# Linear attention into a soft mixture of experts on one core: a batch's second half in other PSUM banks, a batch's keys one tile later, and the drain's zero products in another bank

## The chip, the cores and the metric

The kernel runs on one core of one Trainium2 chip. The metric is device microseconds (us) of one execution. All inputs and the output are float32 and lie in HBM. The host only rearranges the inputs before the launch and the output after it; all arithmetic is on the core.

## The reference

The first part is linear attention without a softmax, for 8 batches and 8 heads, with 576 positions and a head width of 64. Its output is normalised per position and head. The second part is a soft mixture of 8 experts with 4 slots each (32 slots) over all 4608 rows of 512 values.

```python
kv  = einsum('bhsd,bhse->bhde', k, v)
out = einsum('bhsd,bhde->bhse', q, kv)
x   = out / sqrt(mean(out*out, -1) + 1e-6) * g_norm      # to 4608 x 512
logits = x @ phi                                          # 4608 x 32
d = exp(logits - logits.max(0)); d /= d.sum(0)            # over rows
slot_in  = d.T @ x                                        # 32 x 512
slot_out = relu(slot_in[e] @ w1[e]) @ w2[e]               # 4 slots of each expert
c = exp(logits - logits.max(1)); c /= c.sum(1)            # over slots
result = c @ slot_out
```

The softmax over rows needs the maximum of each slot's column over all 4608 rows, so the slot inputs are complete only when the last row tile has its logits. The experts can't start before that.

## The kernel before

**Loads.** All loads and stores are issued by SyncE (SP) in one order: per batch two 1 MB tiles of keys and values (`kv`, L59), 256 KB with the last 64 positions (`kvr`, L63), then the queries (`q`, L70; `qr`, L68), then the expert weights `w1` (L86; some in four parts, L82) and `w2` (L91). The 1 MB tiles share a ring of 17 buffers (`ring`), so a later weight load waits in SP's queue until the tile that used its buffer has been consumed: the weights of experts 6 and 7 and the late halves of `w2` take buffers of the first experts' weights. Each load also uses one of eight completion semaphores in turn, so a load isn't issued before the one eight places ahead of it has landed.

**Stage 1, the row tiles.** The loop over `T` takes 36 tiles of 128 rows, nine for two batches. `products(T)` (L211) multiplies the queries by a block-diagonal matrix `bd` of the batch (there are two, `bds[0]` and `bds[1]`, for even and odd batches) into a PSUM tile `o` of two banks; there are two such tiles under the tag `o`. ScalarE (ACT) squares and evicts it (L237, L244, L245), VectorE (DVE) reduces (L250, L304) and does a Newton step (L266 to L268), GpSimd (POOL) scales (L277, L299). Two tiles make a stage; six tiles make a group, whose column maximum (L317), spread over partitions by TensorE (`pm`, L327) and reduced (L333), feeds the running softmax (`pb`, L342; `d`, L348 and L349) and the weighted sums `pS` (L361).

**The keys.** `class Kv` (L142) makes `bd` of one batch: products of keys and values (L159), the last 64 positions (L174), a copy to SBUF (`kvT`, L183), a transpose and a product with phi (L188, L190), and copies into `bd` (L194 on ACT; L202 on DVE for batch 0, L204 on ACT for the others). All of it uses one PSUM tile of two banks under the tag `kv`, of which there is one. Batch 0 is made ahead of the loop in two halves `g`, each from one of its 1 MB tiles. For every other batch the three steps of `kv_step` (L374) are spread over three iterations: products of the first tile, products of the second tile with the last positions, then the transposes and copies. They stand ahead of `products(T)` in the iterations `first[b] - 3` to `first[b] - 1`. For batch 1 `first` is 4, so these are iterations 1, 2 and 3.

**Order.** The schedule is the program order on each engine; nothing reorders it. Every engine works through its own list, so an instruction that waits holds all that stand behind it on that engine.

**The drain.** After the loop the last two tiles `A` and `Z` go through with smaller steps (L455 to L517). The last group's maximum is the gate: L317 on DVE, `pm` on TensorE, `rmax` (L333) on DVE, `diag` (L337) on ACT, `pb`, `d`, `pS`, the accumulator (L368), its transpose `psT` (L501), `sTe` (L505), then the first expert product `ph` (L564). `tail_ps` is a PSUM tile of two banks under the tag `kv`; the roots of the last two stages are kept in its first bank.

**Zero products.** `fill(n)` (L396) puts `n` bf16 products of zeros, 128 by 256, on TensorE; nobody reads them. They stand at the start (`EARLY`) and in the drain (`LATE_FILL`). Before the drain they go to a new tile of tag `o`; in the drain to the second bank of `tail_ps`. The tag `m` is one bank, used in turn by `pm`, `pb` and `psT`.

**Stage 2.** Experts (L559, L578), the combine weights on DVE (L535), then for each of two halves of the columns a mixing step (L594) and six output tiles (L603), each stored by one DMA of 768 KB (L621).

Of the kernel before, what the change touches and what calls it, by code (L numbers as in the profile page):

```python
# [8 lines left out]
F32 = mybir.dt.float32  # L9
# [5 lines left out]
P = 128  # L15
B, H, S, D = 8, 8, 576, 64
# [9 lines left out]
CT = 12  # L26
NCH = NT // CT
NX = 14
EARLY = (18, 2, 2)
LATE_FILL = (24, 5, 5, 2, 2)  # L30
PACED = 3
SLOT = 2048
NSLOT = 17
# [8 lines left out]
def soft_moe_linear_attention(ctx: ExitStack, tc: tile.TileContext, kv_in, kvr_in, q_in, qr_in, w1_in, w2_in, c_in, out):  # L42


    nc = tc.nc
# [61 lines left out]
    zeros = const.tile([P, 256], BF16, name="zeros")  # L107
# [17 lines left out]
    for i in range(NX):  # L125
        t = const.tile([P, 4, 129], F32, name=f"x{i}")
# [12 lines left out]
    ps = psA.enter_context(tc.tile_pool(name="psA", bufs=1, space=bass.MemoryType.PSUM))  # L139


    class Kv:  # L142


        def __init__(self, b):
            self.b = b
            self.bd = bds[b % 2]
            t = ps.tile([P, 2, 512], F32, tag="kv", name=f"kvp{b}")
            self.pkv = t[:, :, :128].rearrange("p w (g d) -> p w g d", g=2)
            self.pT = t[:, 0, 128:384].rearrange("p (g n) -> p g n", g=2)  # L150
            self.pM = t[:, 1, 128:384].rearrange("p (g h w n) -> p g h w n", g=2, h=2, w=2)

        def products(self, r):
            g, w = divmod(r, 2)
            main = kv_sb[self.b, g].rearrange("p (r w c n) -> p r w c n", r=2, w=2, c=4)
            for c in range(4):
                for i in range(2):
                    lo = 64 * i
                    nc.tensor.matmul(  # L159
                        self.pkv[lo : lo + 64, w, g],  # L160
                        lhsT=main[:, w, 1, c, lo : lo + 64],
                        rhs=main[:, w, 0, c, lo : lo + 64],
                        start=c == 0 and (g == 0 or self.b == 0),
                        stop=False,
                    )
# [66 lines left out]
    def square(T, o):  # L232
        s = stage_of[T]
        if T == starts[s]:
            sqs[s] = wk.tile([P, STAGES[s], 4, P], F32, tag="sq", name=f"sq{s}")

        nc.scalar.activation(sqs[s][:, T - starts[s]], o[:, :, 32:160], AF.Square, scale=0.125)  # L237

    def evict(T, o):
        s = stage_of[T]  # L240
        if T == starts[s]:
            parts[s] = wk.tile([P, STAGES[s], H, NS], F32, tag="part", name=f"part{s}", bufs=3)
        part = parts[s][:, T - starts[s]].rearrange("p (j w) n -> p j w n", w=2)
        nc.scalar.copy(part, o[:, :, :192].rearrange("p j (c n) -> p j c n", n=NS)[:, :, 0::5])  # L244
        nc.scalar.copy(xts[T % NX][:, :, :128], o[:, :, 32:160])  # L245
# [8 lines left out]
    def root(s, home=None):  # L254
        r0 = home
        if r0 is None:
            r0 = wk.tile([P, STAGES[s] * H], F32, tag="r0", name=f"r0{s}")
        nc.scalar.activation(r0, mss[s], AF.Ln, bias=eps)  # L258
        nc.scalar.activation(r0, r0, AF.Exp, scale=-0.5)
        r0s[s] = r0  # L260
# [36 lines left out]
    def scale_part(s, engine):  # L297
        part = parts[s]
        engine.tensor_tensor(  # L299
            out=part, in0=part, in1=rs_of[s].unsqueeze(3).to_broadcast([P, STAGES[s], H, NS]), op=ALU.mult  # L300
        )

    def logits(s):
        nc.vector.tensor_reduce(  # L304
            out=L[:, pos(starts[s]) : pos(starts[s]) + STAGES[s]],
            in_=parts.pop(s).rearrange("p t h n -> p t n h"),
            axis=AX.X,
            op=ALU.add,
        )
# [5 lines left out]
    def group_max(G):  # L315
        at = pos(g0[G])
        nc.vector.tensor_reduce(  # L317
            out=L[:, at + GROUPS[G]],
            in_=L[:, at - (G > 0) : at + GROUPS[G]].rearrange("p t n -> p n t"),
            axis=AX.X,  # L320
            op=ALU.max,
        )

    def group_max_T(G):
        pm = ps.tile([P, P], F32, tag="m", name=f"pm{G}")
        for j in range(4):
            nc.tensor.matmul(  # L327
                pm[32 * j : 32 * j + 32], lhsT=L[:, pos(g0[G]) + GROUPS[G]], rhs=ident, start=True, stop=True
            )
        pms[G] = pm  # L330

    def group_max_row(G):
        nc.vector.tensor_reduce(out=run_max[G % 2], in_=pms.pop(G), axis=AX.X, op=ALU.max)  # L333

    def group_diag(G):
        diag = wk.tile([P, NS], F32, tag="diag", name=f"diag{G}", bufs=1)
        nc.scalar.activation(diag, ident[:, :NS], AF.Copy, scale=run_max[G % 2])  # L337
        held[G] = diag
# [5 lines left out]
    def group_exp(G):  # L344
        n = GROUPS[G]
        pb = pbs.pop(G)
        d = wk.tile([P, n, NS], F32, tag="d", name=f"d{G}")
        nc.vector.tensor_sub(d, L[:, pos(g0[G]) : pos(g0[G]) + n], pb.unsqueeze(1).to_broadcast([P, n, NS]))  # L348
        nc.scalar.activation(d, d, AF.Exp)  # L349
        ds[G] = d  # L350
        if G > 0:
            alphas[G] = wk.tile([P, 1], F32, tag="alpha", name=f"alpha{G}")
            nc.scalar.activation(alphas[G], run_max[G % 2], AF.Exp, scale=-1.0, bias=run_max[(G - 1) % 2])
# [18 lines left out]

    first = {b: 9 * (b // 2) + 4 * (b % 2) for b in range(B)}
    kvs = {}  # L374

    def kv_step(b, i):
        if i == 0:
            kvs[b] = Kv(b)
            kvs[b].products(0)
            kvs[b].products(1)  # L380
        elif i == 1:
            kvs[b].products(2)
            kvs[b].products(3)
            kvs[b].borders((0, 1))
        else:
            kvs[b].slots((0, 1))
# [5 lines left out]
    def group_done(s):  # L392

        return last_of.get(starts[s + 1] - 1)

    def fill(n, cols=256):  # L396

        t = tail_ps or ps.tile([P, 2, 512], F32, tag="o", name="fill", bufs=2)
        for i in range(n):
            nc.tensor.matmul(t[:, 1, :cols], lhsT=zeros[:, :P], rhs=zeros[:, :cols], start=True, stop=True)  # L400

    tail_ps = None
    fill(EARLY[0])
    kvs[0] = Kv(0)
    for g in range(2):
        kvs[0].products(2 * g)
        kvs[0].products(2 * g + 1)
        kvs[0].borders((g,))
        kvs[0].slots((g,))
        fill(EARLY[1 + g])  # L410
    T_at, diag_at, pb_at, d_at, sums_at = {}, {}, {}, {}, {}
    for T in range(NT - 2):
        for b in range(1, B):
            at = T - first[b] + 3
            if 0 <= at < 3:
                kv_step(b, at)
        o = products(T)
        s = ends.get(T - 1)
        if s is not None:
            root(s)  # L420
        if T in diag_at:
            group_diag(diag_at[T])
        square(T, o)
        G = d_at.get(T)
        if G is not None:
            group_exp(G)
            sums_at[T + 1] = G
        evict(T, o)
        old = ends.get(T - 2)
        if old is not None:  # L430
            logits(old)
            if (n := group_done(old)) is not None:
                group_max(n)
                T_at[T + 1] = n
        if T in T_at:
            group_max_T(T_at[T])
            diag_at[T + 1] = pb_at[T + 2] = T_at[T]
        if s is not None:
            newton(s)
        if T in T_at:  # L440
            group_max_row(T_at[T])
        if s is not None:
            scale_part(s, nc.gpsimd)
            scale_x(s)
        if T in pb_at:
            group_exp_PE(pb_at[T])
            d_at[T + 1] = pb_at[T]
        if T in ends:
            mean_square(ends[T])
        if T in sums_at:  # L450
            todo_sums += [(sums_at[T], i) for i in range(GROUPS[sums_at[T]])]
        for _ in range(min(2, len(todo_sums))):
            group_sum(*todo_sums.pop(0))

    s, G = len(STAGES) - 1, len(GROUPS) - 1  # L455
    tail_ps = ps.tile([P, 2, 512], F32, tag="kv", name="tail")
# [23 lines left out]
    group_max(G)  # L480
    for i in todo_sums:
        group_sum(*i)
    fill(LATE_FILL[0])
    group_max_T(G)
    group_max_row(G)
    group_diag(G)
    scale_o(A, oA, True)
    fill(LATE_FILL[1])
    group_exp_PE(G)
    group_exp(G)  # L490
    scale_o(Z, oZ, True)
    fill(LATE_FILL[2])
    for i in range(GROUPS[G]):
        group_sum(G, i)
    fill(LATE_FILL[3])


    sTe = wk.tile([P, NE * 4 * NS], F32, tag="sq", name="sTe")
    nc.gpsimd.memset(sTe, 0.0)
    psT = ps.tile([P, P], F32, tag="m", name="psT")  # L500
    nc.tensor.transpose(psT, acc[:, :128], ident)  # L501
    fill(LATE_FILL[4])
    mine = psT.rearrange("p (j e k) -> p e j k", j=4, k=SPE)
    last = NE - 1
    nc.vector.tensor_scalar_mul(  # L505
# [15 lines left out]
    ps = ctx.enter_context(tc.tile_pool(name="psB", bufs=3, space=bass.MemoryType.PSUM, reuse_waits="tile"))  # L521
# [183 lines left out]
```

## Time and profile before

| | |
|---|---|
| median of three runs | 178.07 us (177.19 to 178.8) |
| the profiled execution's own time | 179.42 us |
| its span in the profile | 177.6 us |
| TensorE matmul busy | 151.7 us (85%) |
| VectorE, ScalarE, GpSimd busy | 88.7, 87.0, 56.0 us |
| moved by DMA | 71.69 MB, mean 404 GB/s |
| HBM read, written | 61.93 MB, 9.44 MB |

Times in the profile run from the start of the span. PE is TensorE's matmuls, PEld its weight loads, SPq is SyncE's queue of DMA issues. A row of the timeline has the start, the duration, the engine, the line, the operation with its output and inputs, the number of merged instructions, and in brackets how long the engine had idled and what released it. A float32 matmul counts as two instructions there. In the view by windows, PEclk is the granted TensorE clock (1.00 is full), and the last two columns are the busy share of the 16 DMA engines and what they moved. The view of DMA issues gives for the issues within a window the median time from issue to landing.

### The profile page before, as it was taken

Reading aid. Unit: us, or ns where it says so; the run is one execution under the profiler, and the core shown is the slowest. Engines: PE = TensorE matmul, PEld = TensorE weight load, DVE = VectorE, ACT = ScalarE, POOL = GpSimd, SP = SyncE. Lnnn points to the kernel's source line nnn. Section 1 sums busy time; section 2 is a strip of 40 time slices with the busy share of each in tenths; the row PEclk is TensorE's granted clock in tenths of the full one; section 3 lists DMA queues with packets and bytes.
Section 4 is the critical chain, followed back from the end, with each engine's and each line's share of the span. In section 5 each row is a group of like instructions: output and inputs, shape, how many; then the busy total and the mean of one; then the engine's idle time right before and its main releaser. Section 6 shows DMA issues by size and latency. Waiting matters only on the chain.

```text
span 177.6 us, 4899 instructions
## 1 busy us (share of the span) xinstructions
PE 151.7 (85%) x2038; PEld 111.3 (63%) x2038; DVE 88.7 (50%) x180; ACT 87.0 (49%) x224; POOL 56.0 (31%) x78
## 2 busy tenths in 40 slices
PE   7676999999989899999999763979979997996910
PEld 5465978989779788888996653656545642433400
DVE  1110255566486565467653679342887313455630
ACT  2113486886957957868778651012222211343510
POOL 7000066656556666265665565000000000000000
PEclk9997899999999999999999999699999999999995
DMA  5999999999999999999999999996999999998996
GB/s 190 417 437 410 426 428 417 430 417 422 426 421 414 428 416 427 422 428 424 426 422 428 422 428 408 419 370 187 435 417 430 417 432 421 424 418 362 378 428 271
DMA packets 12982, 71.69 MB, mean 404 GB/s; under 512 B 1440, under 2 KB 1568, under 8 KB 6176
## 3 DMA queue, kind: packets, MB, share of 16 engines
q1 hardware_dynamic: 12960, 71.37, 97.1%
q8 instruction: 16, 0.26, 0.5%
q14 instruction: 6, 0.05, 0.1%
HBM read 61.93 MB, written 9.44 MB: 402 GB/s over the span
## 4 chain that ended last, share of the span: by engine, by line
PE 47%; DMA 22%; ACT 11%; DVE 10%; issue 3%; POOL 2%; SPq 1%; POOLq 0%; DVEq 0%
PE o L227 18%; DMA w<-in_w_dram 15%; PE kvp L159 9%; DMA kv<-in_kv_dram 7%; PE po L610 6%; PE tail L400 2%; DVE logits L304 2%; PE pS L361 2%; DVE ms L250 2%; POOL part L299 2%; ACT bd L194 2%; PE o L218 2%; PE pY L582 2%; ACT sq L237 2%; DVE st L620 2%
## 5 line engine op out<-in xcount | busy, mean ns | idle before, releaser
L227 PE MATMUL o<-bd,q 128*128 128x192 f32 x256 | 50.6, 341 | 1.5 <-ACT x L245 0.6
L227 PEld LDWEIGHTS o<-bd,q 128*128 128x128 f32 x256 | 41.8, 194 | 4.7 <-ACT x L245 1.6
L277 POOL TENSOR_TENSOR x<-x,r 128x512 f32<-128x512 f32 x34 | 34.7, 1042 | 0.0
L299 POOL TENSOR_TENSOR part<-part,r 128x512 f32<-128x512 f32 x17 | 17.8, 1047 | 52.3 <-DVE r L268 52.3
L304 DVE TENSOR_REDUCE logits<-part 128x64 f32<-128x512 f32 (+1 forms) x19 | 19.2, 1012 | 16.1 <-POOL part L299 16.0
L250 DVE TENSOR_REDUCE ms<-sq 128x16 f32<-128x1024 f32 (+1 forms) x19 | 22.0, 1157 | 10.6 <-ACT sq L237 10.6
L237 ACT ACTIVATE sq<-o 128x512 f32<-128x512 f32 x36 | 21.4, 595 | 10.9 <-PE o L227 10.4
L159 PE MATMUL kvp<-kv 128*64 128x64 f32 x512 | 19.0, 229 | 3.1 <-DMA kv<-in_kv_dram 2.0
L159 PEld LDWEIGHTS kvp<-kv 128*64 128x64 f32 x512 | 16.8, 141 | 6.5 <-issue 3.7
L245 ACT COPY x<-o 128x512 f32<-128x512 f32 x34 | 20.7, 608 | 0.0
L618 ACT COPY st<-po 128x768 f32<-128x768 f32 x12 | 9.3, 800 | 17.6 <-PE po L610 10.2
L582 PE MATMUL pY<-w,x 128*32 128x256 f32 x256 | 16.2, 382 | 1.2 <-DVE x L576 1.2
L620 DVE COPY st<-po 128x768 f32<-128x768 f32 x12 | 11.3, 956 | 8.4 <-PE po L610 7.3
L610 PE MATMUL po<-logits,z 32*128 32x384 f32 x96 | 13.5, 525 | 2.3 <-DVE z L601 1.1
L564 PE MATMUL ph<-w,sTe 128*32 128x256 f32 x224 | 13.0, 379 | 0.3 <-DVE sTe L505 0.3
L582 PEld LDWEIGHTS pY<-w,x 128*32 128x32 f32 x256 | 7.5, 109 | 8.6 <-issue 2.6
L244 ACT COPY part<-o 128x256 f32<-128x256 f32 x34 | 12.6, 371 | 0.0
L361 PE MATMUL pS<-x,d 128*32 128x129 f32 x288 | 10.7, 276 | 2.1 <-ACT d L349 2.1
L258 ACT ACTIVATE r<-ms,eps 128x16 f32<-128x16 f32 x17 | 5.2, 308 | 12.7 <-DVE ms L250 12.5
L610 PEld LDWEIGHTS po<-logits,z 32*128 32x128 f32 x96 | 5.7, 183 | 9.1 <-ACT st L618 3.8
L400 PEld LDWEIGHTS <-zeros 128*128 128x128 bf16 x60 | 7.2, 125 | 6.4 <-issue 3.5
L564 PEld LDWEIGHTS ph<-w,sTe 128*32 128x32 f32 x224 | 7.2, 110 | 5.2 <-DVE sTe L505 0.6
(79 smaller groups left out, 142.0 us busy)
## 6 DMA issues: line engine op xcount, KB each, us to landing
w<-in_w_dram SPq DMA_DIRECT2D x29, 1024.0 KB, 17.7
kv<-in_kv_dram SPq DMA_DIRECT2D x16, 1024.0 KB, 14.3
out_dram<-st SPq DMA_DIRECT2D x12, 768.0 KB, 4.8
q<-in_qt_dram SPq DMA_DIRECT2D x8, 1024.0 KB, 14.2
kvr<-in_kr_dram SPq DMA_DIRECT2D x8, 256.0 KB, 14.8
x<-in_w_dram SPq DMA_DIRECT2D x8, 256.0 KB, 7.2
qr<-in_qr_dram SPq DMA_DIRECT2D x4, 256.0 KB, 13.7
w<-in_w_dram SPq DMA_DIRECT2D x4, 256.0 KB, 15.0
```

The source lines that it names most:

```text
L159: nc.tensor.matmul(self.pkv[lo : lo + 64, w, g], lhsT=main[:, w, 1, c, lo : lo + 64], rhs=main[:, w, 0, c, lo : lo + 64], start=c == 0 and ...
L227: nc.tensor.matmul(o[:, r, :192], lhsT=q_sb[2 * g + i][:, r, at : at + P], rhs=bds[i][:, r], start=True, stop=True)
L237: nc.scalar.activation(sqs[s][:, T - starts[s]], o[:, :, 32:160], AF.Square, scale=0.125)
L245: nc.scalar.copy(xts[T % NX][:, :, :128], o[:, :, 32:160])
L250: nc.vector.tensor_reduce(out=mss[s], in_=sqs.pop(s).rearrange("p t j (w d) -> p (t j w) d", w=2), axis=AX.X, op=ALU.add)
L277: nc.gpsimd.tensor_tensor(out=x, in0=x, in1=r[:, i].rearrange("p (j w) -> p j w", w=2).unsqueeze(3).to_broadcast([P, 4, 2, D]), op=ALU.mult,)
L299: engine.tensor_tensor(out=part, in0=part, in1=rs_of[s].unsqueeze(3).to_broadcast([P, STAGES[s], H, NS]), op=ALU.mult)
L304: nc.vector.tensor_reduce(out=L[:, pos(starts[s]) : pos(starts[s]) + STAGES[s]], in_=parts.pop(s).rearrange("p t h n -> p t n h"), axis=AX ...
L564: nc.tensor.matmul(ph[32 * j : 32 * j + 32], lhsT=sTe[:, (4 * e + c) * NS : (4 * e + c + 1) * NS], rhs=w1[c % 2][j], start=c == 0, stop=c ...
L582: nc.tensor.matmul(pY[32 * j : 32 * j + 32, hf, :256], lhsT=hTs[e][:, c], rhs=w2[:, c], start=e == 0 and c < 4, stop=e == NE - 1 and c >= 4,)
L610: nc.tensor.matmul(po[:, u, : CT * NS].rearrange("p (g x) -> p g x", g=2), lhsT=z[lo : lo + 32, f * P : (f + 1) * P], rhs=cT[k][lo : lo + 32],
L620: nc.vector.tensor_copy(out=st[:, 2:4], in_=po[:, :, : CT * NS])
```

## The change

It has three parts and two counts of zero products.

1. Batch 0's second half gets a `Kv` of its own, whose PSUM tile has the tag `o` instead of `kv`. The first half keeps the tag `kv`.
2. Batch 1's steps 0 and 1 both stand ahead of tile 2; its step 2 stays ahead of tile 3. Nothing stands ahead of tile 1 any more. All other batches keep their places.
3. The first block of zero products of the drain goes to a new tile of tag `m`; the four other blocks stay in `tail_ps`.
4. That block has 28 products instead of 24, and the two zero products after batch 0's second half are dropped.

On TensorE the start of batch 0's second half stood like this; `kvp` is the PSUM tile of the keys, `kv_1` the second 1 MB tile of batch 0, and the names in brackets are what the instruction waits for (DMAHW is a load's landing, Activation is ScalarE):

```order
L400 MATMUL fill<-zeros 128x256
L159 MATMUL kvp_221<-kv_1_75 64x64 [waits DMAHW3_49,DVE_49,Activation_49]
L159 MATMUL kvp_221<-kv_1_75 64x64 x15
L174 MATMUL kvp_221<-kvr_70 64x64 x4
L188 MATMUL kvp_221<-ident,kvT_1_273 128x128 [waits Activation_49]
```

In the changed kernel, with the tile of tag `o`:

```order
L404 MATMUL fill<-zeros 128x256
L159 MATMUL kvp_o<-kv_1_75 64x64 [waits DMAHW3_49,PE_49]
L159 MATMUL kvp_o<-kv_1_75 64x64 x15
L174 MATMUL kvp_o<-kvr_70 64x64 x4
L188 MATMUL kvp_o<-ident,kvT_1_274 128x128 [waits Activation_49]
```

The wait for DVE and ScalarE, which read the first half's results out of the old tile, is gone; the wait for the load stays.

On TensorE the first tiles of the loop stood in this order (`o` are the outputs of tiles 0, 1 and 2, `kv_0_80` and `kv_1_82` the two tiles of batch 1, `kvr_79` its last positions):

```order
L227 MATMUL o_284<-bd_163,q_77 128x192 x4
L159 MATMUL kvp_294<-kv_0_80 64x64 x16
L227 MATMUL o_311<-bd_163,q_77 128x192 x4
L159 MATMUL kvp_294<-kv_1_82 64x64 x16
L174 MATMUL kvp_294<-kvr_79 64x64 x8
L227 MATMUL o_347<-bd_163,q_77 128x192 x4
```

and now stand in this one:

```order
L227 MATMUL o_282<-bd_163,q_77 128x192 x4
L227 MATMUL o_292<-bd_163,q_77 128x192 x4
L159 MATMUL kvp_kv<-kv_0_80 64x64 x16
L159 MATMUL kvp_kv<-kv_1_82 64x64 x16
L174 MATMUL kvp_kv<-kvr_79 64x64 x8
L227 MATMUL o_345<-bd_163,q_77 128x192 x4
```

Tile 1 has moved ahead of both key tiles of batch 1.

In the drain, TensorE's rows from the last sums of the group before (`pS`) to the first zero product were these:

```order
L361 MATMUL pS_1423<-x_169,d_1385 32x129 [waits Pool_49]
L361 MATMUL pS_1423<-x_169,d_1385 32x129 x3
L400 LDWEIGHTS zeros
L400 MATMUL tail<-zeros 128x256 [waits DVE_49]
L400 LDWEIGHTS zeros
```

and are now:

```order
L361 MATMUL pS_1421<-x_169,d_1383 32x129 [waits Pool_49]
L361 MATMUL pS_1421<-x_169,d_1383 32x129 x3
L404 LDWEIGHTS zeros
L404 MATMUL fill<-zeros 128x256 [waits DVE_49]
L404 LDWEIGHTS zeros
```

Both wait for DVE, but for other readers of other tiles: the old one for the last reader of `tail_ps` (L268 of the last stage), the new one for the last reader of the bank `m`, which is the subtraction of `pb` (L348) of the group before. `pm` follows the zero products in both.

The diff:

```diff
--- before.py
+++ after.py
@@ -26,8 +26,8 @@
 CT = 12
 NCH = NT // CT
 NX = 14
-EARLY = (18, 2, 2)
-LATE_FILL = (24, 5, 5, 2, 2)
+EARLY = (18, 2, 0)
+LATE_FILL = (28, 5, 5, 2, 2)
 PACED = 3
 SLOT = 2048
 NSLOT = 17
@@ -142,10 +142,10 @@
     class Kv:
 
 
-        def __init__(self, b):
+        def __init__(self, b, tag="kv", bufs=None):
             self.b = b
             self.bd = bds[b % 2]
-            t = ps.tile([P, 2, 512], F32, tag="kv", name=f"kvp{b}")
+            t = ps.tile([P, 2, 512], F32, tag=tag, name=f"kvp{b}_{tag}", bufs=bufs)
             self.pkv = t[:, :, :128].rearrange("p w (g d) -> p w g d", g=2)
             self.pT = t[:, 0, 128:384].rearrange("p (g n) -> p g n", g=2)
             self.pM = t[:, 1, 128:384].rearrange("p (g h w n) -> p g h w n", g=2, h=2, w=2)
@@ -372,6 +372,8 @@
 
     first = {b: 9 * (b // 2) + 4 * (b % 2) for b in range(B)}
     kvs = {}
+    kv_steps = {(b, i - 3): (i,) for b in range(2, B) for i in range(3)}
+    kv_steps.update({(1, -2): (0, 1), (1, -1): (2,)})
 
     def kv_step(b, i):
         if i == 0:
@@ -393,26 +395,27 @@
 
         return last_of.get(starts[s + 1] - 1)
 
-    def fill(n, cols=256):
-
-        t = tail_ps or ps.tile([P, 2, 512], F32, tag="o", name="fill", bufs=2)
+    def fill(n, cols=256, home=None):
+
+        if not n:
+            return
+        t = home if home is not None else ps.tile([P, 2, 512], F32, tag="o", name="fill", bufs=2)[:, 1]
         for i in range(n):
-            nc.tensor.matmul(t[:, 1, :cols], lhsT=zeros[:, :P], rhs=zeros[:, :cols], start=True, stop=True)
-
-    tail_ps = None
+            nc.tensor.matmul(t[:, :cols], lhsT=zeros[:, :P], rhs=zeros[:, :cols], start=True, stop=True)
+
     fill(EARLY[0])
-    kvs[0] = Kv(0)
+
     for g in range(2):
-        kvs[0].products(2 * g)
-        kvs[0].products(2 * g + 1)
-        kvs[0].borders((g,))
-        kvs[0].slots((g,))
+        kv = Kv(0, "o" if g else "kv", 2 if g else None)
+        kv.products(2 * g)
+        kv.products(2 * g + 1)
+        kv.borders((g,))
+        kv.slots((g,))
         fill(EARLY[1 + g])
     T_at, diag_at, pb_at, d_at, sums_at = {}, {}, {}, {}, {}
     for T in range(NT - 2):
         for b in range(1, B):
-            at = T - first[b] + 3
-            if 0 <= at < 3:
+            for at in kv_steps.get((b, T - first[b]), ()):
                 kv_step(b, at)
         o = products(T)
         s = ends.get(T - 1)
@@ -480,26 +483,26 @@
     group_max(G)
     for i in todo_sums:
         group_sum(*i)
-    fill(LATE_FILL[0])
+    fill(LATE_FILL[0], home=ps.tile([P, 256], F32, tag="m", name="fill"))
     group_max_T(G)
     group_max_row(G)
     group_diag(G)
     scale_o(A, oA, True)
-    fill(LATE_FILL[1])
+    fill(LATE_FILL[1], home=tail_ps[:, 1])
     group_exp_PE(G)
     group_exp(G)
     scale_o(Z, oZ, True)
-    fill(LATE_FILL[2])
+    fill(LATE_FILL[2], home=tail_ps[:, 1])
     for i in range(GROUPS[G]):
         group_sum(G, i)
-    fill(LATE_FILL[3])
+    fill(LATE_FILL[3], home=tail_ps[:, 1])
 
 
     sTe = wk.tile([P, NE * 4 * NS], F32, tag="sq", name="sTe")
     nc.gpsimd.memset(sTe, 0.0)
     psT = ps.tile([P, P], F32, tag="m", name="psT")
     nc.tensor.transpose(psT, acc[:, :128], ident)
-    fill(LATE_FILL[4])
+    fill(LATE_FILL[4], home=tail_ps[:, 1])
     mine = psT.rearrange("p (j e k) -> p e j k", j=4, k=SPE)
     last = NE - 1
     nc.vector.tensor_scalar_mul(
```

## The prediction

> **What bounds the kernel now.** I read four views: the busy time by windows, the timeline of TensorE at both ends of stage 1, the waits of SP's queue, and the DMA issues with their landings. First the middle of stage 1:
>
> ```profile
> 26.00:50.00 24.00, 23.91 (x310) 20.34 (x306) 14.50 (x28) 19.23 (x54) 14.35 (x15) 1.00 1.01 419
> 75.00:95.00 20.00, 19.97 (x294) 17.14 (x291) 12.11 (x23) 15.63 (x45) 11.64 (x12) 1.00 1.01 425
> ```
>
> TensorE (the second number) is busy nearly without a gap and the DMA engines are full as well. From 26 to 95 us nothing can be won or given back; a start that is earlier by some time reaches the drain earlier by that time. The loads run ahead of it, held back only by the ring. So the question is where transfers stop, because the last store ends the kernel:
>
> ```profile
> 118.00:120.00 2.00, 1.51 (x29) 0.74 (x24) 0.84 (x4) 0.00 (x0) 0.00 (x0) 1.00 0.90 331
> 120.00:122.00 2.00, 2.00 (x40) 1.23 (x43) 0.21 (x2) 0.05 (x1) 0.00 (x0) 1.00 0.25 83
> 122.00:124.00 2.00, 2.00 (x44) 1.18 (x36) 0.45 (x1) 0.80 (x2) 0.00 (x0) 1.00 0.93 258
> ...
> SPq L86 <- PE ph L564: 4.7, 4, 3.4
> ```
>
> The last column falls to 331, 83 and 258 GB/s against 425 before. That is (94 + 342 + 167) / 425 x 2 us = 2.8 us of transfer lost. The wait says why: L86, the weights of experts 6 and 7, stands in SP's queue for 3.4 us until the first expert product (`ph`, L564) frees a buffer of the ring. That product waits for the drain's chain, so the drain's end restarts the transfers. What follows, from the queue's timeline and the landings:
>
> ```profile
> 116.90 0.33 SPq L82 DMA_DIRECT2D x<-in_w_dram  x1
> 121.03 2.92 SPq L86 DMA_DIRECT2D w<-in_w_dram  x4
> ...
> x<-in_w_dram SPq DMA_DIRECT2D x1, 256.0 KB, 5.3
> ...
> w<-in_w_dram SPq DMA_DIRECT2D x1, 1024.0 KB, 4.8
> ...
> 121.89 0.33 SPq L86 DMA_DIRECT2D w<-in_w_dram  x1
> ...
> w<-in_w_dram SPq DMA_DIRECT2D x1, 1024.0 KB, 7.8
> ...
> 134.68 0.33 SPq L91 DMA_DIRECT2D w<-in_w_dram  x1
> ...
> w<-in_w_dram SPq DMA_DIRECT2D x1, 1024.0 KB, 19.4
> ...
> 164.16 7.15 SPq L621 DMA_DIRECT2D out_dram<-st  x6
> ...
> out_dram<-st SPq DMA_DIRECT2D x1, 768.0 KB, 3.2
> ```
>
> The landing rows belong to the issues in their order (5.3 to 116.90, 4.8 to the first of the four at 121.03, 7.8 to 121.89, 19.4 to 134.68, 3.2 to the first of the six stores at 164.16). The last load ahead of the gap lands at 116.90 + 5.3 = 122.2. The first load behind it lands at 121.03 + 4.8 = 125.8, the second at 121.89 + 7.8 = 129.7, the last weight load, ten later, at 134.68 + 19.4 = 154.1: 2.44 us each for these ten. The seventh store lands at 164.16 + 3.2 = 167.4, so seven stores took 13.3 us, 1.9 each. From the restart to the end the transfers are back to back. Without the gap the twelve loads would end at 122.2 + 12 x 2.44 = 151.5, that is 2.6 us earlier. **So however early the drain ends, the kernel gains about 2.7 us** (2.6 by the landings, 2.8 by the lost bytes), as long as the drain ends at least that much earlier.
>
> **The start.**
>
> ```profile
> 2.11 0.43 SPq L59 DMA_DIRECT2D kv<-in_kv_dram  x1
> ...
> kv<-in_kv_dram SPq DMA_DIRECT2D x1, 1024.0 KB, 6.8
> ...
> 3.07 0.91 SPq L59 DMA_DIRECT2D kv<-in_kv_dram  x2
> ...
> kv<-in_kv_dram SPq DMA_DIRECT2D x1, 1024.0 KB, 14.0
> ...
> 9.36 1.15 PE L159 MATMUL kvp<-kv 128*64 128x64 f32 x32 [1.06 <-DVE bd L202]
> ...
> 12.97 0.89 PE L227 MATMUL o<-bd,q 128*128 128x192 f32 x4 [0.34 <-DVE bd L202]
> 15.34 1.69 PE L159 MATMUL kvp<-kv 128*64 128x64 f32 x32 [1.49 <-DMA kv<-in_kv_dram]
> 16.96 2.62 PE L227 MATMUL o<-bd,q 128*128 128x192 f32 x8
> ...
> 20.99 1.57 PE L227 MATMUL o<-bd,q 128*128 128x192 f32 x8
> ...
> 25.26 1.49 PE L218 MATMUL o<-bd,qr 128*64 128x192 f32 x14 [0.27 <-ACT bd L204]
> ```
>
> Batch 0's second half waited until 9.36 for DVE's copies out of the shared tile. Its load, issued at 2.11, landed at 8.9. With its own banks it starts there: 0.45 us gained. The two zero products dropped behind it are worth nothing: TensorE waits for DVE there anyway, 0.34 us ahead of 12.97. Tile 0's second part then ends at 13.86 - 0.45 = 13.4. Tile 1 comes next instead of the idle 1.49 us; at the 1.5 us that tile 2 takes it ends at 14.9, ahead of batch 1's first load, which still lets TensorE go at 15.34. Products of that load 1.1 us, to 16.4. Then TensorE is idle until the second load, issued as the second of the pair at 3.07 (some 3.55) and landing 14.0 later, at 17.5. The step that moves back issues products on TensorE alone, no copy and no DMA, and passes only tile 1. Queued behind the new wait are the second products, the last positions, tile 2 and all later tiles: 1.1 + 0.4 us, so tile 2 starts at 19.05 instead of 20.99, **1.9 us gained**. ScalarE's squares and copies of tile 2 and batch 1's `bd` follow tile 2, so tile 4, which waited for `bd` at 25.26, goes at about 23.3. Part of this is the clock:
>
> ```profile
> 12.32:15.73 3.41, 1.59 (x19) 1.06 (x20) 0.45 (x2) 1.36 (x4) 0.00 (x0) 1.00 0.99 411
> 15.73:19.14 3.41, 3.41 (x34) 3.29 (x30) 0.00 (x0) 0.00 (x0) 0.00 (x0) 0.50 1.05 429
> 111.30:114.72 3.42, 3.42 (x23) 2.06 (x21) 0.77 (x2) 0.00 (x0) 0.00 (x0) 0.50 1.02 417
> ```
>
> After 3.41 us with only 1.59 busy the granted clock was 0.50 for the next 3.41 us, and tile 1 took 2.62 us. With tile 1 in the first window it is busy some 3.0, so that loss goes. The second window then holds 2.3 us of work; were that too little, tiles 2 and 3 would take 2.6 us instead of 1.5 and the start would lose 0.3 instead of gaining 1.9. That is the low end. The Trainium skill ("TensorE: Matmul & The Clock Gate", What's actually happening) lets the clock fall only after a whole idle window of about 3.4 us; by it the low end could not occur, but it also leaves the 0.50 here unexplained, after idle times of 1.49 and 2.74 us, so the trace decides.
>
> **The drain.**
>
> ```profile
> 104.99 0.35 DVE L348 TENSOR_TENSOR d<-logits,pb 128x192 f32<-128x192 f32 x1
> ...
> 109.93 0.16 DVE L268 SCALAR_TENSOR_TENSOR r<-r,tail 128x8 f32<-128x8 f32 x1
> ...
> 111.28 0.53 DVE L317 TENSOR_REDUCE logits<-logits 128x32 f32<-128x224 f32 x1
> ...
> 114.97 0.29 DVE L333 TENSOR_REDUCE rmax<-pm 128x1 f32<-128x128 f32 x1 [2.90 <-PE pm L327]
> ...
> 105.88 1.53 PE L361 MATMUL pS<-x,d 128*32 128x129 f32 x48 [1.71 <-ACT d L349]
> 110.14 4.20 PE L400 MATMUL tail<-zeros 128*128 128x256 bf16 x24 [2.74 <-DVE r L268]
> 114.27 0.62 PE L327 MATMUL pm<-ident,logits 128*32 128x128 f32 x8
> 114.82 0.72 PE L400 MATMUL tail<-zeros 128*128 128x256 bf16 x5
> ```
>
> The group's maximum was ready at 111.8, but `pm` stood behind 24 zero products that could start only at 110.14, when DVE's last read of `tail_ps` was done, and so came at 114.27. In the bank `m` the block waits for the subtraction of `pb`, done at 105.3, so it starts right behind the sums, at 107.4. Its 28 products at 0.72 / 5 = 0.144 us take 4.0 us, to 111.4: `pm` goes at 111.85, when the maximum is there. That is 2.4 us, and up to 0.3 more if `pm`, which took 0.62 under the halved clock of 111.30 to 114.72, runs at the full one. At 4.20 / 24 = 0.175 us each the block ends at 112.3 and the gain is 1.9. I take **2.5 us** (range 1.9 to 2.7). What is late next is DVE's own row of work up to L317, which the change doesn't touch.
>
> **The sum.** The first expert product comes 1.9 + 2.5 = 4.4 us earlier (between 1.6 and 4.6: the low ends are -0.3 and 1.9, the high ones 1.9 and 2.7), of which the transfers let 2.7 through. The loads needed next can follow:
>
> ```profile
> 127.07 0.33 SPq L91 DMA_DIRECT2D w<-in_w_dram  x1
> ...
> w<-in_w_dram SPq DMA_DIRECT2D x1, 1024.0 KB, 17.3
> ...
> 146.34 1.07 PE L582 MATMUL pY<-w,x 128*32 128x256 f32 x16
> ```
>
> The tightest lands at 144.4 for a product at 146.34, 1.9 us of room; the product moves 4.4 and the load 2.6, so the room is just used up. The profiled execution's 177.6 us of span and 179.42 us become 174.9 and 176.7. The median of the runs lies 1.35 us below that execution; 178.07 - 2.7 = **175.3 us**.
>
> **Rivals.** (a) Only one of the two ends gains. The drain alone gives 2.5 us, 175.6, hardly to be told from the forecast; the start alone 1.9, 176.2. For it speaks the uncertain clock in the start; against it, that the two places share no wait. (b) The transfers don't cap, and the whole 4.4 us arrive: 173.7. For it speaks that store seven was issued at 164.16 only when its data was there; against it, that it landed 1.9 us behind six stores that followed the weights without a gap. By the Trainium skill ("DMA: Bandwidth & Descriptors", Where 436 GB/s comes from) the ceiling is 435 GB/s, 2% above the 425 here: an estimate of some 1.2 us over the 51 us after the restart, so it allows part of it. (c) Less of the gap closes. The first load behind it landed 125.8 - 122.2 = 3.6 us after the load ahead of it, 1.2 more than a load takes; another 1.5 came only between the first and the second (3.9 instead of 2.44). If those 1.5 us are no part of the gap, some engine having been held up for another reason, they come again and the gain is 1.2 us: 176.9. For it speaks that the queue was well filled by then; against it, that the three windows up to 124 us already lost 2.8 us over all engines. (d) Slower: the halved clock spreads from the start into the loop. With batch 1's keys bunched, TensorE waits at 16.4 and again for `bd` ahead of tile 4, and a TensorE that is slow from there on leaves the engines behind it out of step, so that more windows are less than half full. Each halved window costs 1.1 us (tile 1's 2.62 against 1.5). Four of them eat the 4.4 us, which is the point from which it decides; with six the kernel is 2.2 us slower, 180.3. For it speaks that 1.59 of 3.41 us busy was enough to halve the clock; against it, that the loop keeps TensorE busy for 23.91 of 24 us, so that a halved window mends itself in the next.
>
> **How the numbers follow.** The forecast has 0.62, (a) 0.15, (b) 0.08, (c) 0.11, (d) 0.04. The predicted time is that of the forecast. A change of 1% (1.8 us) is about what a measurement can tell from none. Faster by more: the forecast, (b), most of (a), 0.80; within 1%: (c), the rest of (a) and the small cases of (d), 0.17; slower 0.03. The range reaches from 174.0, short of (b), which is left out with (d), to 177.0, which takes in (a) and (c).
>
> **What would show it.** The window with 83 GB/s gone, `pm` at the end of L317 without a wait behind zero products, tile 1 ahead of batch 1's first products and no 0.50 around 16 to 19 us, TensorE idle near 17 us. Expert products should start more than 4 us earlier and the first store by as much, while the last moves by 2.7. The forecast is wrong if the last store moves as far as the expert products, or if the dip in transfers stays.

## The result and the profile after

The changed kernel takes 177.0 us (median of 20 runs, 176.47 to 177.91) against 178.06 us (20 runs, 176.97 to 179.85). The ratio is 0.9945, with a 95% interval of 0.9921 to 0.9968: 0.55% faster, within the 1% that the prediction called no change. A ratio, here and below, leaves out runs more than 1.5% above the fastest of the same kernel, in this comparison three of the old kernel's, 179.68 to 179.85 us; the profile before, at 179.42 us, was of a run nearly as long. The profiled execution after took 176.62 us, with a span of 174.8 us.

The windows of the changed kernel around the old gap:

```profile
118.00:120.00 2.00, 2.00 (x44) 1.23 (x40) 0.45 (x1) 0.47 (x1) 0.00 (x0) 1.00 1.06 351
120.00:122.00 2.00, 2.00 (x44) 1.23 (x40) 1.07 (x3) 0.47 (x1) 0.00 (x0) 1.00 1.02 410
122.00:124.00 2.00, 2.00 (x44) 1.17 (x36) 1.31 (x4) 0.65 (x2) 0.00 (x0) 1.00 1.02 418
...
SPq L86 <- PE ph L567: 1.4, 4, 0.5
```

The dip to 83 GB/s is gone; some 0.45 us of transfer is lost instead of 2.8, and SP's longest wait for `ph` is 0.5 us instead of 3.4. The start on TensorE:

```profile
8.89 1.15 PE L159 MATMUL kvp_o<-kv 128*64 128x64 f32 x32 [0.51 <-DMA kv<-in_kv_dram]
...
15.05 1.15 PE L159 MATMUL kvp_kv<-kv 128*64 128x64 f32 x32 [0.34 <-DMA kv<-in_kv_dram]
17.50 1.15 PE L159 MATMUL kvp_kv<-kv 128*64 128x64 f32 x32 [1.30 <-DMA kv<-in_kv_dram]
...
18.97 1.57 PE L227 MATMUL o<-bd,q 128*128 128x192 f32 x8
...
23.24 1.49 PE L218 MATMUL o<-bd,qr 128*64 128x192 f32 x14 [0.27 <-ACT bd L204]
```

Batch 0's second half starts when its load has landed, TensorE then waits 1.30 us for batch 1's second load, and tiles 2 and 4 come 2.0 us earlier (18.97 for 20.99, 23.24 for 25.26). The drain, TensorE first and then DVE's maximum:

```profile
103.89 1.53 PE L361 MATMUL pS<-x,d 128*32 128x129 f32 x48 [1.71 <-ACT d L349]
105.35 3.23 PE L404 MATMUL fill<-zeros 128*128 128x256 bf16 x28
109.98 0.43 PE L327 MATMUL pm<-ident,logits 128*32 128x128 f32 x8 [1.40 <-DVE logits L317]
...
112.50 2.79 PE L361 MATMUL pS<-x,d 128*32 128x129 f32 x48 [0.16 <-ACT d L349]
...
116.66 3.66 PE L567 MATMUL ph<-w,sTe 128*32 128x256 f32 x64 [0.28 <-DVE sTe L508]
...
109.31 0.53 DVE L317 TENSOR_REDUCE logits<-logits 128x32 f32<-128x224 f32 x1
```

`pm` now waits for the maximum, not for zero products. But the 28 products took 3.23 us, TensorE then idled 1.40 us, and the sums `pS`, 1.53 us in the group before, took 2.79. The windows of the clock tell why:

```profile
16.17:19.58 3.41, 2.11 (x54) 1.95 (x53) 0.42 (x1) 0.42 (x2) 0.00 (x0) 1.00 1.04 431
...
108.33:111.74 3.41, 1.90 (x22) 1.14 (x20) 2.71 (x7) 0.32 (x1) 0.00 (x0) 1.00 1.01 400
111.74:115.16 3.42, 3.26 (x52) 2.50 (x49) 0.82 (x2) 0.55 (x2) 0.00 (x0) 0.50 1.02 417
```

The half clock of the start is gone, and the one of the drain fell on another stretch. Behind the drain, the weights and stores:

```profile
117.80 2.05 SPq L86 DMA_DIRECT2D w<-in_w_dram  x3
...
w<-in_w_dram SPq DMA_DIRECT2D x1, 1024.0 KB, 7.0
...
160.93 7.15 SPq L624 DMA_DIRECT2D out_dram<-st  x6
...
out_dram<-st SPq DMA_DIRECT2D x1, 768.0 KB, 3.6
```

The first load behind the old gap lands at 117.80 + 7.0 = 124.8 (125.8 before), the seventh store at 160.93 + 3.6 = 164.5 (167.4 before, 2.9 us earlier).

So the profiled executions differ by 2.8 us, where 2.7 was worked out, and the medians by 1.1. The question for the experiments is where the rest is.

### The profile page after: what moved, and what is told of

The parts are those of the page before. It is cut to its first block, busy times and chain, and to the rows that moved or that the text cites. A ratio compares the mean times of both kernels' runs of the same rounds, so it can differ in the third digit from the quotient of the medians.

```text
span 174.8 us, 4903 instructions
## 1 busy us (share of the span) xinstructions
PE 150.5 (86%) x2040; PEld 110.5 (63%) x2040; DVE 88.7 (51%) x180; ACT 87.0 (50%) x224; POOL 56.0 (32%) x78
## 4 chain that ended last, share of the span: by engine, by line
PE 52%; DVE 16%; ACT 12%; DMA 8%; issue 4%; POOL 2%; SPq 1%; POOLq 0%; DVEq 0%
PE o L227 17%; PE kvp_kv L159 8%; DMA kv<-in_kv_dram 8%; PE po L613 6%; PE ph L567 6%; PE pY L585 5%; DVE logits L304 3%; PE pS L361 2%; DVE ms L250 2%; POOL part L299 2%; ACT bd L194 2%; PE o L218 2%; ACT sq L237 2%; DVE st L623 2%; PE kvp_kv L174 2%
## 5 line engine op out<-in xcount | busy, mean ns | idle before, releaser
L227 PE MATMUL o<-bd,q 128*128 128x192 f32 x256 | 49.4, 336 | 1.5 <-ACT x L245 0.6
L227 PEld LDWEIGHTS o<-bd,q 128*128 128x128 f32 x256 | 40.8, 190 | 4.7 <-ACT x L245 1.6
L159 PE MATMUL kvp_kv<-kv 128*64 128x64 f32 x480 | 17.4, 226 | 2.1 <-DMA kv<-in_kv_dram 2.1
L159 PEld LDWEIGHTS kvp_kv<-kv 128*64 128x64 f32 x480 | 15.4, 139 | 5.2 <-DMA kv<-in_kv_dram 3.0
L361 PE MATMUL pS<-x,d 128*32 128x129 f32 x288 | 12.0, 301 | 1.9 <-ACT d L349 1.9
L361 PEld LDWEIGHTS pS<-x,d 128*32 128x32 f32 x288 | 8.5, 119 | 4.5 <-issue 4.0
L575 ACT ACTIVATE h<-ph,rs 128x256 f32<-128x256 f32 x8 | 3.8, 472 | 14.1 <-PE ph L567 14.1
## 6 DMA issues: line engine op xcount, KB each, us to landing
qr<-in_qr_dram SPq DMA_DIRECT2D x4, 256.0 KB, 14.1
```

Of the source, the lines that this page charges most:

```text
L159: nc.tensor.matmul(self.pkv[lo : lo + 64, w, g], lhsT=main[:, w, 1, c, lo : lo + 64], rhs=main[:, w, 0, c, lo : lo + 64], start=c == 0 and ...
L227: nc.tensor.matmul(o[:, r, :192], lhsT=q_sb[2 * g + i][:, r, at : at + P], rhs=bds[i][:, r], start=True, stop=True)
L361: nc.tensor.matmul(pS[32 * j : 32 * j + 32], lhsT=ds[G][:, i], rhs=x[:, j], start=i == 0, stop=i == GROUPS[G] - 1)
```

## The experiments

The theory ("phase") is that the clock is granted in stretches of 3.41 us which begin at another moment of the program in each execution. The half clock in the start and in the drain then falls in some executions only, so the first expert product comes at another time in each, and most executions of the old kernel had less of the gap than the profiled one. Its companion ("cap") is that once the gap is closed the transfers alone set the end. The main rival ("rate") is that every execution has the same gap and the scatter is in the transfers' speed. Three further rivals, "bank", "chain" and "clock", are named where they are tested.

**The old kernel again.** Four more profiles of the kernel before, unchanged; the first also timed.

> The kernel before, unchanged, timed against itself. Theory 'phase': the clock is granted in stretches of 3.41 us whose start differs from execution to execution, so the half clock near 16 us and near 111 us does not fall in every execution, the gap in the transfers is 2.8 us only where both fall, and the runs spread by about 2.5 us (177.0 to 179.8), the ones with the lower mean clock (0.967 or less) being the longer ones. Rival 'rate': all executions have the same gap and differ in how fast the transfers run elsewhere; then time and mean clock are unrelated. Ratio to itself 1.000 by both.

> The kernel before, unchanged, one more profile. Theory 'phase': if its time is 1 us or more under 179.4, the windows between 116 and 124 us lose correspondingly less than 2.8 us of transfer and at least one of the two stretches of half clock is missing or lies elsewhere. Rival 'rate': the windows lose 2.8 us again, and the shorter time comes from more GB/s in the other windows.

> The kernel before, unchanged, one more profile. Theory 'phase': its time follows the start of the first expert product: about 177.2 for 117, 177.7 for 118, 179.4 for 119.9 us; with one stretch of half clock (in the start or in the drain, not in both) the product starts between 117.5 and 119 us and the time is 177.5 to 178.5. Rival 'rate': no such relation.

> The kernel before, unchanged, one more profile, with the same expectations: by 'phase' the time follows the start of the first expert product, by 'rate' it doesn't.

The four executions took 177.41, 177.65, 179.58 and 178.10 us; against itself the ratio is 1.0008 (0.9981 to 1.0034). Rows of TensorE and three windows of `same_1` (177.41 us):

```profile
15.77 1.15 PE L159 MATMUL kvp<-kv 128*64 128x64 f32 x32 [1.86 <-DMA kv<-in_kv_dram]
16.85 1.57 PE L227 MATMUL o<-bd,q 128*128 128x192 f32 x8
...
19.82 1.57 PE L227 MATMUL o<-bd,q 128*128 128x192 f32 x8
...
108.97 2.78 PE L400 MATMUL tail<-zeros 128*128 128x256 bf16 x24 [2.74 <-DVE r L268]
...
117.10 1.27 PE L564 MATMUL ph<-w,sTe 128*32 128x256 f32 x18 [0.28 <-DVE sTe L505]
...
118.00:120.00 2.00, 2.00 (x44) 1.23 (x40) 0.34 (x1) 0.47 (x1) 0.00 (x0) 1.00 1.20 341
120.00:122.00 2.00, 2.00 (x44) 1.23 (x40) 0.77 (x3) 0.47 (x1) 0.00 (x0) 1.00 0.83 277
122.00:124.00 2.00, 2.00 (x44) 1.18 (x37) 1.35 (x3) 0.55 (x1) 0.00 (x0) 1.00 1.02 411
```

The same program, and even more idle time ahead of batch 1's keys (1.86 us, 1.49 in the profile before), but tile 1 takes 1.57 us and not 2.62, and the 24 zero products 2.78 and not 4.20: no half clock in either place. Tile 2 starts at 19.82 instead of 20.99. The first expert product comes at 117.10 instead of 119.89, and the lost transfer is (84 + 148 + 14) / 425 x 2 = 1.2 us instead of 2.8. The same rows of `same_3` (179.58 us) and three windows:

```profile
17.44 2.29 PE L227 MATMUL o<-bd,q 128*128 128x192 f32 x8
...
110.28 4.45 PE L400 MATMUL tail<-zeros 128*128 128x256 bf16 x24 [2.73 <-DVE r L268]
...
120.07 1.29 PE L564 MATMUL ph<-w,sTe 128*32 128x256 f32 x20 [0.28 <-DVE sTe L505]
...
15.53:18.94 3.41, 3.41 (x37) 3.29 (x38) 0.00 (x0) 0.00 (x0) 0.00 (x0) 0.50 1.02 416
111.10:114.51 3.41, 3.41 (x18) 2.32 (x16) 1.06 (x3) 0.00 (x0) 0.00 (x0) 0.50 1.04 421
120.00:122.00 2.00, 1.93 (x36) 1.20 (x40) 0.39 (x4) 0.00 (x0) 0.00 (x0) 1.00 0.24 90
```

This is the profile before once more: half clock in both places, 90 GB/s. The two half clocks begin 111.10 - 15.53 = 95.57 us apart, and so they do in the profile before (111.30 - 15.73): 95.57 / 28 = 3.413 us, so 28 whole stretches. Within an execution the stretches thus follow each other without a shift; against the program they lie elsewhere in each. In `same_4` (178.10 us) TensorE ran slowly from the beginning (batch 0's first products took 1.98 us, 1.15 in `same_1`), and tile 0 came late; the drain was at full clock:

```profile
5.71 1.98 PE L159 MATMUL kvp<-kv 128*64 128x64 f32 x32 [0.64 <-DMA kv<-in_kv_dram]
...
14.69 2.63 PE L227 MATMUL o<-bd,q 128*128 128x192 f32 x8
...
110.47 2.78 PE L400 MATMUL tail<-zeros 128*128 128x256 bf16 x24 [2.74 <-DVE r L268]
...
118.60 2.78 PE L564 MATMUL ph<-w,sTe 128*32 128x256 f32 x45 [0.28 <-DVE sTe L505]
```

`same_2` (177.65 us) was slow at the beginning in the same way, and its drain too was at full clock; the three windows from 118 to 124 us lose 1.2 us in it and 1.5 in `same_4`. The rate between 126 and 151 us was 422 to 424 GB/s in all of them, so "rate" falls. In 89 timed executions of the old kernel, from these comparisons, the mean granted clock of an execution orders the times:

| mean clock | executions | lowest, median, highest us |
|---|---|---|
| 0.980 or more | 26 | 176.65, 177.12, 178.59 |
| 0.971 to 0.979 | 26 | 177.60, 177.95, 178.38 |
| under 0.971 | 37 | 177.87, 178.16, 179.91 (13 above 179) |

The mean clock doesn't hold the slow beginning: `same_2` and `same_4` have 0.983 and 0.984, and the view by windows shows 1.00 where their products took 1.98 us. So the first row has such executions too, and it reaches up to 178.59.

**One half of the change at a time.** In `start_only` the drain is as before; in `drain_only` the start is.

```diff
 # start_only: the changed kernel, but
-LATE_FILL = (28, 5, 5, 2, 2)
+LATE_FILL = (24, 5, 5, 2, 2)
-    fill(LATE_FILL[0], home=ps.tile([P, 256], F32, tag="m", name="fill"))
+    fill(LATE_FILL[0], home=tail_ps[:, 1])
 # drain_only: the changed kernel, but
-EARLY = (18, 2, 0)
+EARLY = (18, 2, 2)
-    kv_steps = {(b, i - 3): (i,) for b in range(2, B) for i in range(3)}
-    kv_steps.update({(1, -2): (0, 1), (1, -1): (2,)})
+    kv_steps = {(b, i - 3): (i,) for b in range(1, B) for i in range(3)}
-        kv = Kv(0, "o" if g else "kv", 2 if g else None)
+    # one kv = Kv(0) ahead of the loop over g
```

> The changed start (parts 1 and 2, two zero products dropped), the drain as before. Theory 'phase': the start's half clock is gone in every execution, the first expert product comes about 2 us earlier than in the profile of the kernel before, the gap shrinks to under 1 us, the median falls by 0.5 to 1.0 us and the longest runs (over 179 us) vanish. Rival 'rate': the gap shrinks by 1.9 us in every execution, the median falls by 1.9 us.

> The changed drain (part 3 and 28 zero products), the start as before. Theory 'phase': the first expert product comes 2 to 3 us earlier, which nearly closes the gap in every execution; the median falls by 0.7 to 1.0 us, about as far as with the whole change. Rival 'rate': the median falls by 2 us or more.

`start_only` took 177.41 us (176.93 to 178.78): its median fell by 0.55 us, the runs above 179 us are gone, and the profiled one lost 0.9 us of transfer, all as "phase" has it. The ratio, 0.9994 (0.9968 to 1.0021), can't tell it from no gain. `drain_only` took 176.94 us (176.75 to 177.66; ratio 0.9962, 0.9941 to 0.9984), all that the whole change brings. TensorE's rows, first of `start_only`:

```profile
108.37 4.11 PE L404 MATMUL tail<-zeros 128*128 128x256 bf16 x24 [2.73 <-DVE r L268]
...
117.83 0.42 PE L567 MATMUL ph<-w,sTe 128*32 128x256 f32 x4 [0.28 <-DVE sTe L508]
```

and of `drain_only`:

```profile
106.31 3.23 PE L403 MATMUL fill<-zeros 128*128 128x256 bf16 x28
...
116.36 1.93 PE L566 MATMUL ph<-w,sTe 128*32 128x256 f32 x32 [0.28 <-DVE sTe L507]
```

In this execution of `start_only` the 24 products ran under a half clock as in the profile before (4.11 us, 4.20 there), so the first expert product comes 2.1 us earlier, which is the start's part alone. In that of `drain_only` it comes 3.5 us earlier, enough to close the gap; but 1.0 of these were there before the drain, since its start had no half clock (`pS` of the group before at 104.85, 105.88 in the profile before).

**Nothing of the change, but TensorE kept busy.** `warm_start` and `warm_both` add zero products to the old kernel where TensorE idles; all else stays.

```diff
 # warm_start: the kernel before, in the loop
     for T in range(NT - 2):
+        if T == 1:
+            warm = ps.tile([P, 256], F32, tag="m", name="warm")
+            for _ in range(9):
+                nc.tensor.matmul(warm, lhsT=zeros[:, :P], rhs=zeros, start=True, stop=True)
 # warm_both: also, in the drain
+    warm = ps.tile([P, 256], F32, tag="m", name="warm2")
+    for _ in range(22):
+        nc.tensor.matmul(warm, lhsT=zeros[:, :P], rhs=zeros, start=True, stop=True)
     fill(LATE_FILL[0])
```

> The kernel before with nine more zero products ahead of batch 1's first products, in the 1.5 to 1.9 us in which TensorE waits there, in the bank of the maximum; they compute nothing that is read. Theory 'phase': the half clock near 16 us is gone in every execution, the runs above 179.5 us vanish, the median falls by 0.2 to 0.5 us, since only the executions with a half clock in both places lose the whole 2.8 us. Rival 'rate': nothing moves, and the runs above 179.5 us stay.

> The same with 22 more zero products in the drain, in the 2.7 us in which TensorE waits ahead of its 24, which stay in their bank and still start where they did. Nothing of the change is in it but TensorE kept busy. Theory 'phase': no half clock before 120 us, all runs lie where the unchanged kernel's shortest do, 176.8 to 177.5, the median falls by 0.7 to 1.0 us: what the change gained is the clock's part, not the bank's. Rival 'bank': the 24 products still hold the spread of the maximum by 0.9 us or more behind the maximum itself, and the median falls by less than 0.4 us.

`warm_start`: 177.17 us (ratio 0.996, 0.993 to 0.9989), its median 0.87 us lower where 0.2 to 0.5 was expected. `warm_both`: 176.97 us (ratio 0.9921, 0.989 to 0.9952), the changed kernel's time without the change. Ten of its twelve runs lie between 176.73 and 177.09 us. The other two, at 179.8 and 180.0, and one of `warm_start`'s at 180.7 had a mean clock of 0.977 to 0.979, so "phase" doesn't explain them. The drain of `warm_both` on TensorE:

```profile
105.98 2.58 PE L489 MATMUL warm<-zeros 128*128 128x256 bf16 x22
108.80 2.78 PE L400 MATMUL tail<-zeros 128*128 128x256 bf16 x24 [0.25 <-DVE r L268]
...
116.93 2.37 PE L571 MATMUL ph<-w,sTe 128*32 128x256 f32 x40 [0.28 <-DVE sTe L512]
```

The 24 products still start only after L268 and still stand ahead of `pm`. As "bank" had it, `pm` still comes 1.0 us behind the maximum (at 111.51, L317 ended at 110.48), yet the median falls by 1.07 us, where "bank" allowed less than 0.4. So "bank" falls as the only cause.

**No zero products at all ahead of the maximum.** `no_block` is the kernel before with `LATE_FILL = (0, 5, 5, 2, 2)`.

> The kernel before without its 24 zero products in the drain, so nothing stands ahead of the spread of the maximum, and nothing keeps the clock up. Theory 'phase': the spread of the maximum follows the maximum at once, 0.9 to 2.5 us earlier, but the clock is halved behind it in many executions, which stretches the sums and more, 1.3 us or more; median 177.5 to 178.3. Rival 'bank': the hold was the whole cost and the median falls to 177.0, as with the change.

```profile
110.43 0.60 PE L327 MATMUL pm<-ident,logits 128*32 128x128 f32 x8 [4.54 <-DVE logits L317]
110.96 1.25 PE L400 MATMUL tail<-zeros 128*128 128x256 bf16 x5
...
113.47 1.74 PE L361 MATMUL pS<-x,d 128*32 128x129 f32 x48
...
116.59 3.66 PE L564 MATMUL ph<-w,sTe 128*32 128x256 f32 x64 [0.28 <-DVE sTe L505]
```

177.20 us (10 runs, 176.63 to 178.32; ratio 0.9982, 0.9954 to 1.001): nearer to what "bank" expected. The half clock came as foreseen (five products in 1.25 us instead of 0.72) but stretched the chain by less than the 24 products had held it. The profiled executions but those of `late` and `late44` sort by the time from the start of the sums `pS` of the group before to the start of the first expert product:

| ahead of `pm` | clock in the drain | us | executions |
|---|---|---|---|
| nothing that holds it | full | 11.5 | drain_only, fill40 (below) |
| 24 products in `tail_ps` | full | 12.4 | same_1, same_2, same_4, warm_start, warm_both |
| nothing that holds it | half | 12.2, 12.8 | no_block, changed kernel |
| 24 products in `tail_ps` | half | 13.7 to 14.1 | start_only, profile before, same_3 |

The old place of the zero products costs 0.9 us at the full clock, and the half clock 0.7 to 1.7 us. So in the old kernel the block and the clock together made the delay, and taking away either is enough, because the cap leaves no more to win.

**The cap.** Three variants of the changed kernel move the first expert product and little else: 40 zero products in the drain's first block (`fill40`), and 21 or 44 more right ahead of `ph` (`late`, `late44`).

```diff
-LATE_FILL = (28, 5, 5, 2, 2)
+LATE_FILL = (40, 5, 5, 2, 2)     # fill40
+LATE_FILL = (28, 5, 5, 2, 23)    # late
+LATE_FILL = (28, 5, 5, 2, 46)    # late44
```

> The changed kernel with 40 zero products instead of 28 in the drain's first block: 28 took 3.23 us and left TensorE idle for 1.40 us ahead of the spread of the maximum, and the clock was then halved, which stretched the sums from 1.53 to 2.79 us. Theory 'cap': no half clock in the drain, the first expert product 1.0 to 1.3 us earlier, and the time unchanged within 0.3 us, because the transfers have no gap left to close. Rival 'chain': 1 us less.

> The changed kernel with 21 more zero products right ahead of the first expert product, which then comes some 2.2 us later (21 x 0.116 less 0.3 us of wait). Theory 'cap': the changed kernel has its transfers nearly without a gap and has room, so the median rises by 1.0 to 1.5 us only, and the windows from 116 to 124 us lose some 1.5 us more of transfer than in the changed kernel. Rival 'chain': the chain of compute sets the end and the median rises by 2.2 us.

> The changed kernel with 44 more zero products right ahead of the first expert product, which then starts at about 119.9 us, where the kernel before had it in its slowest execution, but with the clock full all the way. Theory 'phase' with 'cap': it is the start of the first expert product alone that counts, so the gap in the transfers is back at 2 to 3 us and the median is 178.8 to 179.6. Rival 'clock': the half clock itself cost the time elsewhere, and the median stays under 178.3.

`fill40`: 177.02 us (176.71 to 177.48); its product starts at 115.89, 0.8 us before that of the changed kernel (1.0 to 1.3 expected), and nothing is gained. `late`: 177.41 us (177.06 to 181.84, two of its twelve runs above 179), 0.4 more, less than the 1.0 to 1.5 expected, since its product came at 117.52, only 0.9 us after the changed kernel's, whose profile had a half clock. `late44`: 179.74 us (four runs, 179.59 to 181.67; ratio to before 1.014, 1.0078 to 1.0202), just above the 178.8 to 179.6 expected, and this with the clock full in every window:

```profile
114.98 5.19 PE L404 MATMUL tail<-zeros 128*128 128x256 bf16 x46
120.10 1.28 PE L567 MATMUL ph<-w,sTe 128*32 128x256 f32 x19
...
120.00:122.00 2.00, 2.00 (x38) 1.19 (x40) 0.00 (x0) 0.00 (x0) 0.00 (x0) 1.00 0.27 98
```

The dip is back at 98 GB/s. "Chain" falls with `fill40`, "clock" with `late44`. All profiled executions in a row, by the start of the first expert product and the execution's own time:

| execution | `ph` starts | us |
|---|---|---|
| fill40 | 115.89 | 177.22 |
| drain_only | 116.36 | 177.66 |
| no_block | 116.59 | 177.12 |
| changed kernel | 116.66 | 176.62 |
| warm_both | 116.93 | 176.92 |
| warm_start | 116.99 | 177.19 |
| same_1 | 117.10 | 177.41 |
| late | 117.52 | 177.25 |
| start_only | 117.83 | 177.65 |
| same_2 | 118.14 | 177.65 |
| same_4 | 118.60 | 178.10 |
| profile before | 119.89 | 179.42 |
| same_3 | 120.07 | 179.58 |
| late44 | 120.10 | 179.63 |

Up to about 117.5 us no effect of the start shows within the scatter, and the time is 176.6 to 177.7; behind that it rises by (179.63 - 177.25) / (120.10 - 117.52) = 0.9 us for each us. `same_3` and `late44`, one with two stretches of half clock and the other with none, agree within 0.05 us: a late first expert product costs the same, whatever delayed it.

## Why the prediction was wrong

- **What bounds the kernel.** Right. The gap hangs on the first expert product, it closed, and the transfers cap the gain. The sign that was named for this is weak in the pair itself, where the expert products moved by 3.2 us and the end by 2.8; `fill40` and `late44` show it.
- **The cap of 2.7 us.** Right for the execution it was read from: a span of 174.9 and 176.7 us were worked out, 174.8 and 176.62 came. `late44`, the last row of the table, shows the same from the other side: with the gap back the time is that of the profile before.
- **The start, 1.9 us.** Right against that execution: 2.0, with the 1.30 us wait at 17.5 us where it was expected, and no half clock after a window with 2.11 us busy. But 1.2 of these 2.0 us were that execution's half clock: in `same_1` the old kernel's tile 2 came at 19.82, only 0.85 behind the changed kernel's.
- **The drain, 2.5 us.** The mechanism was right. `pm` moved by 4.29 us, 2.0 of them from the start, so 2.3; 1.4 of these were again the half clock (the 24 products took 4.20 us, 2.78 in `same_1`). The mis-sized term was the zero products, 0.144 us each from a row of five; 28 took 3.23 us, 0.115 each. The block therefore left TensorE idle for 1.40 us ahead of `pm`, the clock fell again in that execution, and the first expert product came 3.2 us earlier instead of 4.4. The cap hid it, as `fill40` showed.
- **The step that failed** is the last of the sum: "The median of the runs lies 1.35 us below that execution; 178.07 - 2.7 = 175.3 us". It took the difference for an offset of the measurement and the 2.7 us for something that every run loses. But the 1.35 us were part of the 2.7: the median run had the first expert product earlier and less of a gap. Of the five profiled executions of the old kernel two had the half clock in both places; the middle one, `same_4`, started `ph` at 118.60, took 178.10 us and lost 1.5 us of transfer. With the clock full in both places (`same_1`) `ph` started at 117.10, where hardly anything is left to gain. A cap is a level, not a difference: once the transfers run without a gap, hardly an execution is shorter than 176.5 us, and 26 of the old kernel's 89 executions, those with a mean clock of 0.980 or more, already have a median of 177.12. Had the cap been set against the runs as a level, 176.7 us would have been the forecast, 0.3 us from the measured median and within 1% of the median before.
- **The rivals.** None had this. (c) came near the measured time, 176.9, but for another reason, a gap that doesn't close; it closed. Both ends gained, so (a) did not happen, nor did (b) and (d); behind 126 us the changed kernel's rate was 424 GB/s, 422 in the profile before.
- The three runs given, 177.19, 178.07 and 178.8, and the profiled execution at 179.42 already spread by 2.2 us where the changed kernel's 20 runs spread by 1.4; the spread was itself the sign that the stall differed from run to run.

The Trainium skill ("TensorE: Matmul & The Clock Gate", What's actually happening) says that the clock's window is 3413 ns and free-running, so that it doesn't begin with the kernel. The traces agree with that: the half clock began at 15.73 us in the profile before, at 15.53 in `same_3`, and not at all in the start of `same_1`. The prediction used the page's rule for the idle time and passed over this one, by which the two half clocks need not fall in every run.

What stays open: the remaining scatter of 176.6 to 177.7 us, where the product starts before 117.5, doesn't follow the first expert product and has no cause here: `drain_only` took 177.66 us with its product at 116.36. Nor have the six long runs of `warm_start`, `warm_both`, `late` and `late44`, 179.4 to 181.8 us, of which only `late`'s two had a low mean clock (0.969 and 0.958).

## What to carry to other kernels

Before a stall of one profiled execution is subtracted from a median, look whether the runs scatter, and whether the stall hangs on something that differs from run to run, as a granted clock does. Where a second resource caps a gain, work out the level it caps at and hold it against the shortest runs of before: if some already reach it, the change removes scatter and little more. Nine zero products in an idle stretch gained as much in the median as the changed start (177.17 and 177.41 us), so try the cheapest way of holding the clock first.

## What the runs showed of the hardware

The clock fell to one half after stretches of 3.41 us in which TensorE's matmuls were busy for 0.13 us (`no_block`), 0.82 and 1.47 (`same_3`), 1.16 and 1.59 (the profile before) and 1.36 (`start_only`), but also after one with 1.90 (108.33 to 111.74 in the changed kernel), while it stayed full after 1.53 (the profile before), 1.66 and 1.93 (`same_1`) and 2.11 (the changed kernel). So an idle time of 1.4 to 2.7 us can be enough, but need not be: the same 1.40 us ahead of `pm` left the clock full in `drain_only` and `late44`. The busy time of matmuls alone does not draw the line. Rows of three of these, of the profile before, of `same_1` and of `start_only`:

```profile
104.48:107.89 3.41, 1.53 (x48) 1.38 (x49) 2.71 (x10) 1.94 (x6) 2.65 (x3) 1.00 1.00 423
```

```profile
11.91:15.32 3.41, 1.66 (x10) 1.10 (x8) 0.45 (x2) 1.81 (x5) 0.00 (x0) 1.00 1.01 418
```

```profile
104.28:107.70 3.42, 1.36 (x48) 1.18 (x41) 2.90 (x7) 1.26 (x5) 3.13 (x4) 1.00 1.01 426
107.70:111.12 3.42, 2.75 (x14) 1.95 (x14) 2.31 (x8) 0.03 (x1) 0.00 (x0) 0.50 0.99 405
```
